# A delta-rule scan fed into a two-layer MLP on one core: the down products of the middle token groups turned round, one PSUM bank for the up products, four banks for the scan's pieces, and the last stores from two queues

## The chip, the cores and the metric

The kernel runs on one core of a Trainium2 chip. The metric is device microseconds of one execution, the median of several; lower is better. The engines are TensorE (PE in the profile; PEld is its weight load), VectorE (DVE), ScalarE (ACT), GpSimd (POOL) and SyncE (SP), which issues most of the DMAs.

## The reference

Four batches of eight heads run a delta rule over 768 steps with a state of 48x48. The outputs, 3072 tokens of 384 numbers, go through an MLP with 2048 hidden units.

```python
k_n = k / (np.linalg.norm(k, axis=-1, keepdims=True) + 1e-06)
for t in range(S):
    y[:, :, t] = einsum('bhd,bhde->bhe', q[:, :, t], state)
    v_old = einsum('bhde,bhd->bhe', state, kt)
    state = state + bt[:, :, :, None] * einsum('bhd,bhe->bhde', kt, vt - v_old)
x = y.transpose(0, 2, 1, 3).reshape(B * S, H * D)        # 3072 x 384
h = x @ w_in                                             # 384 -> 2048
g = np.where(h >= 1, h, np.where(h <= -1, 0.0, (h + 1) ** 2 / 4))
return g @ w_out                                         # 2048 -> 384
```

## The kernel before

The scan is cut into 12 chunks of 64 steps, taken in six pairs, G = 0 to 5. For each chunk there are Gram products (`gram_k`, `gram_q`), a triangular solve (16x16 blocks for the first two pairs, `solve_whole` with 30 steps of two DVE instructions, L325 and L327, for the others), merges of the solved blocks (`merge16`, `merge32`), and a chain over the state (`chain_r`, `chain_u`, `chain_y`, `chain_d`). Each of these is called a piece: a batch of some 64 small matmuls, and an eviction of their banks on ACT or DVE.

The MLP works on the 512 tokens of a pair in 16 items, one for each block `f` of 128 hidden units; pair 0 does some blocks in halves of 256 tokens and has 22. An item is:

- up: nine matmuls of 128x512 (three blocks of `x`, each as high x high, high x low and low x high parts in fp32r) into a bank `h`
- the activation, which with s = relu(0.5 - 0.5h), then relu(1 - s), then its square, then max with h gives g: three ACT instructions (L762 twice, L789) and one on DVE (L791)
- the split of g into `ghi` (ACT, L757) and `glo` (DVE, L758)
- down, two items later (`LAG = 2`): twelve matmuls of 128x384, in which the pieces of g are the weights and the block's `w_out` moves, summed over the 16 items in four banks `o0` to `o3`, one for 128 tokens.

The order on every engine is written out by hand. The loop over `items` issues the up products, then the pieces that the table `pe` holds for this half item, then the DVE and ACT work of the table `fill` (solver steps, transposes, loads), then the down products of two items ago, then the second half item's pieces ("late"). `plan(G)` fills both tables; the scan of pair G+1 runs beside the MLP of pair G, and `at(pe, G, 4.5, ...)` means the second half of item 4. An engine carries out its instructions in that order. The solver's steps for pair G+1 stand in the last items of pair G-1 and the first eight of pair G; merges and chain follow.

PSUM has eight banks: two for `h`, four for `o`, and two, called `ch`, for all pieces. When pair 0 starts and before, a ring `spare` lets the pieces use banks that the MLP doesn't need yet.

A finished pair is stored by `store`: four ACT copies and eight DMAs of 64 rows on SP. In the last pair two of the copies are on DVE, and seven of the eight DMAs are on SP, one on ACT's queue.

Of the kernel before, what the change touches and what calls it, by code (L numbers as in the profile page):

```python
# [19 lines left out]
DF = 2048  # L20
FT = DF // 128
# [3 lines left out]
PASSES = ((0, 0), (0, 1), (1, 0))  # L25
# [5 lines left out]
def delta_rule_moe(ctx: ExitStack, tc: tile.TileContext, kqa, kqb, kv, beta, w, out):  # L31
# [27 lines left out]
    ctx.enter_context(tc.manual_schedule())  # L59

    K, KE, GE, Q, KV, XB, RAW, WT = {}, {}, {}, {}, {}, {}, {}, {}
    START = [dict(name=n, bufs=b) for n, b in (("ch", 2), ("ch", 2), ("h", 2), ("h", 2), ("o2", 1), ("o3", 1), ("o0", 1), ("o1", 1))]
    spare = []

    def acc():
# [151 lines left out]
    def gram_q(g):  # L217

        x, b_ = Q[g], banks(C)
        for j in range(H):  # L220
            for e, f in quarters():
                r, o = slice(f * C, f * C + D), other(e, f) * C
                nc.tensor.matmul(b_[e][o:o + C, j], K[g][r, e * H + j, :], x[r, (1 - f, 1)[e], e * H + j, :], start=True, stop=True)  # L223

        def moved():
            for o in range(2):
                yield x[o * C:o * C + C, o, 0:H], b_[0][o * C:o * C + C], slice(o * C, o * C + C)
            yield x[:, 0, H:NU], b_[1], slice(0, P)

        def evict():  # L230
            def raw():
                for a, b, r in moved():
                    nc.scalar.copy(out=a, in_=b)

            def masks(copied=False):
                for a, b, r in moved():
                    nc.vector.tensor_tensor(out=a, in0=a if copied else b, in1=mask[r, None, :].broadcast_to([r.stop - r.start, H, C]), op=ALU.mult)  # L237
                    yield
            return (raw, masks(True)) if g < 2 else lambda: run(masks())
        return evict  # L240
# [387 lines left out]
        return slice(bs[0] * NB, bs[-1] * NB + NB)  # L628

    def up(G, f, bs):  # L630
        h = ps.tile([P, 2 * NB], F32, name="h", bufs=2)
        n = 0
        for k in range(3):
            for x, y in PASSES:
                nc.tensor.matmul(h[:, cols(bs)], WT[f][:, 0, x, k * P:(k + 1) * P], XB[G][:, y, k, cols(bs)], start=(n == 0), stop=(n == 8))  # L635
                n += 1
        return h

    def down(G, f, bs):
        ghi, glo = gs.pop((G, f, bs))  # L640
        for b in bs:
            left[G, b] -= 1
            for k in (2 * b, 2 * b + 1):
# [5 lines left out]
                for n, (x, y) in enumerate(PASSES):  # L649
                    nc.tensor.matmul(oacc[G, k], (ghi, glo)[x][:, k * P:(k + 1) * P], WT[f][:, 1, y, :],  # L650
                                     start=(new and n == 0), stop=(left[G, b] == 0 and n == 2))

    def store(G, b):
        o = sb.tile([P, 2, DM], F32, name="wx", bufs=2)
        for k in (2 * b, 2 * b + 1):
            (nc.scalar.copy, nc.vector.tensor_copy)[k % 2 if G == NS - 1 else 0](out=o[:, k % 2], in_=oacc[G, k])
            for j in range(CT):
                (nc.scalar if G == NS - 1 and k + j == TT else nc.sync).dma_start(out=out.rearrange("(b n t) m -> n b t m", b=CB, t=C)[2 * G + b, k % 2 * CT + j], in_=o[j * C:j * C + C, k % 2])
# [10 lines left out]
    def chain(G, t, a):  # L669
        for j, f, g in ((0, chain_u, a), (0.5, chain_y, a), (1.5, chain_d, a), (2.5, chain_r, a + 1), (3.5, chain_u, a + 1), (4, chain_y, a + 1), (5, chain_d, a + 1)):  # L670
            if (f, g) != (chain_d, ntot - 1):
                at(pe, G, t + j, lambda f=f, g=g: f(g))

    def plan(G):

        a, b = 2 * G + 2, 2 * G + 3
        if G == NS - 1:
            return
        va, vb = scale_v(a), scale_v(b)
        if G == 0:  # L680
# [24 lines left out]
            last = FT + HALF
        else:
            so, un = solves.pop(G)
            at(fill, G, 0.5, (va, 1))
            at(fill, G, 1, (va, 1))
            at(pe, G, 2.5, lambda: chain_r(a))  # L710
            at(pe, G, 4.5, lambda: gram_q(a))
            at(pe, G, 6, lambda: gram_q(b))
            cost, hs = 0, 0
            t, n = (-2.5, 19) if G == 1 else (-1.5, 17)
            for j in range(1, 31):
                at(fill, G, t + hs / 2, (so, 1))
                cost += j * (31 - j) + 150
                hs = int(cost / 9461 * n)
            for j, t in enumerate((7, 7.5, 8, 8)):
                at(fill, G, t, (un, 1))  # L720
            at(fill, G, 9, (vb, 1))
            at(fill, G, 9.5, (vb, 1))
            M = 8.5
            last = 16
        for j, x in ((0, (0, None)), (0.5, (1, 0)), (2.5, (None, 1))):
            at(pe, G, M + j, lambda x=x: merge32(*x))
        chain(G, M + 1.5, a)
        if G < NS - 2:
            if G:
                at(fill, G, 6.5, (load_k, a + 2))  # L730
            at(fill, G, M + 0.5, (load_k, b + 2, (nc.sync, nc.sync), True))
            at(pe, G, M + 1, lambda: gram_k(a + 2))
            at(pe, G, M + 3.5, lambda: gram_k(b + 2))
            lane_steps(G, M + 2, lanes(G + 2), 2.5, 3, 3.5, 4)
            solves[G + 1] = solve_whole(), unlanes_whole()
            at(fill, G, M + 3, (load_q, a + 2))
            at(fill, G, M + 5, (load_k, b + 2))
            at(fill, G, M + 6.5, (load_q, b + 2))
            at(fill, G, last + 0.5, (load_kv, a + 2))
            at(fill, G, last + 1.5, (load_kv, b + 2))  # L740
# [20 lines left out]
    def relu(out, in_, bias, scale):  # L761
        nc.scalar.activation(out=out, in_=in_, func=AF.Relu, bias=bias, scale=scale)  # L762

    late, last, ready = [], None, []
    for n, item in enumerate(items):
        at_, c = 2 * n, cols(item[2])
        finish(late)
        if last:
            rest(*last)
            ready.append(last[0])  # L770
        if at_ == 2 * HALF:
            spare.clear()
        h = up(*item)

        s = sb.tile([P, 2 * NB], F32, name="s", bufs=2)
        relu(s[:, c], h[:, c], mid, -0.5)
        evicts = products(*pe.pop(at_, []))
        run(wu, 3 if n == 0 else 1)
        fills(at_)
        finish(evicts)  # L780
        run(wu, 2 if n < HALF else 1)
        if len(ready) == LAG:
            x = ready.pop(0)
            down(*x)
            for b in x[2]:
                if left[x[0], b] == 0:
                    store(x[0], b)
        relu(s[:, c], s[:, c], one, -1.0)
        nc.scalar.activation(out=s[:, c], in_=s[:, c], func=AF.Square)  # L789
        late = products(*pe.pop(at_ + 1, []))  # L790
        nc.vector.tensor_tensor(out=s[:, c], in0=h[:, c], in1=s[:, c], op=ALU.max)  # L791
# [6 lines left out]
    for b in range(2):  # L798
        gs[G, FT - 1, (b,)] = gs[G, FT - 1, (0, 1)]
        down(G, FT - 1, (b,))  # L800
        store(G, b)

# [1 line left out]
def layouts(q, k, v, beta, moe_w_in, moe_w_out):  # L804
# [43 lines left out]
```

## Time and profile before

| | |
|---|---|
| time, median of 3 runs | 622.01 us (621.1 to 622.45) |
| the profiled execution's own time | 620.85 us |
| its span | 619.1 us |
| mean granted TensorE clock | 0.943 |
| PE busy | 583.6 us, 94% |
| DVE busy | 409.3 us, 66% |
| ACT busy | 393.9 us, 64% |
| time of the 16 DMA engines taken by the queue with most packets | 22.6% |

Durations that the text takes from the profile come from that one execution. A row of a timeline has the start in us from the span's start, the duration, engine, line, operation, names and shapes, and in brackets the idle time before it with what ended it. A row of groups ends with the total busy time and the mean in ns, and the idle time before. The clock is low in the first 100 us and 1.00 from about 120 us on.

### The profile page before, as it was taken

Reading aid. Unit: us, or ns where it says so; the run is one execution under the profiler, and the core shown is the slowest. Engines: PE = TensorE matmul, PEld = TensorE weight load, DVE = VectorE, ACT = ScalarE, POOL = GpSimd, SP = SyncE. Lnnn points to the kernel's source line nnn. Section 1 sums busy time; section 2 is a strip of 40 time slices with the busy share of each in tenths; the row PEclk is TensorE's granted clock in tenths of the full one; section 3 lists DMA queues with packets and bytes.
Section 4 is the critical chain, followed back from the end, with each engine's and each line's share of the span. In section 5 each row is a group of like instructions: output and inputs, shape, how many; then the busy total and the mean of one; then the engine's idle time right before and its main releaser. Section 6 shows DMA issues by size and latency. Waiting matters only on the chain.

```text
span 619.1 us, 21754 instructions
## 1 busy us (share of the span) xinstructions
PE 583.6 (94%) x9562; PEld 511.5 (83%) x9562; DVE 409.3 (66%) x848; ACT 393.9 (64%) x685; POOL 29.8 (5%) x62
## 2 busy tenths in 40 slices
PE   7977967799999999999999999999999999999996
PEld 7966956688888888888888888888888888889995
DVE  4989899972379873379973489954489945333332
ACT  3436775649667569656578646587647586666663
POOL 5110000010010000020000020000020000000000
PEclk9556697999999999999999999999999999999999
DMA  5672756200124210214210224110124000020002
GB/s 141 197 244 71 233 196 202 88 4 3 42 61 119 74 31 3 69 31 125 72 30 8 65 53 119 54 31 24 49 71 124 1 4 16 12 54 1 0 1 51
DMA packets 32831, 42.97 MB, mean 69 GB/s; under 512 B 7152, under 2 KB 27440, under 8 KB 32736
## 3 DMA queue, kind: packets, MB, share of 16 engines
q1 hardware_dynamic: 31600, 39.43, 22.6%
q10 hardware_dynamic: 880, 2.07, 1.0%
q8 instruction: 75, 1.23, 0.8%
q0 software_dynamic: 256, 0.08, 0.1%
q14 instruction: 20, 0.16, 0.1%
HBM read 34.47 MB, written 4.72 MB: 63 GB/s over the span
## 4 chain that ended last, share of the span: by engine, by line
PE 70%; ACT 11%; DVE 9%; SPq 3%; DMA 3%; issue 2%; DVEq 0%; ACTq 0%
PE o L650 27%; PE h L635 27%; PE ch L452 3%; ACT XT L406 2%; ACT GG L404 2%; PE ch L414 2%; ACT s L762 2%; PE ch L223 2%; PE ch L430 1%; ACT XT L399 1%; PE ch L496 1%; PE o L583 1%; PE ch L375 1%; ACT s L789 1%; SPq L484 1%
## 5 line engine op out<-in xcount | busy, mean ns | idle before, releaser
L635 PE MATMUL h<-xb,wt 128*128 128x512 f32 (+1 forms) x918 | 229.1, 395 | 9.1 <-DMA xb<-wt 8.1
L635 PEld LDWEIGHTS h<-xb,wt 128*128 128x128 f32 x918 | 166.8, 195 | 43.2 <-DVE xb L183 4.4
L650 PE MATMUL o<-wt,ghi 128*128 128x384 f32 x768 | 202.1, 344 | 0.1
L791 DVE TENSOR_TENSOR s<-h,s 128x512 f32<-128x512 f32 (+1 forms) x102 | 66.8, 655 | 124.3 <-ACT s L789 123.8
L650 PEld LDWEIGHTS o<-wt,ghi 128*128 128x128 f32 x768 | 137.8, 189 | 7.5 <-issue 0.5
L757 ACT CAST ghi<-s 128x512 fp32r<-128x512 f32 (+1 forms) x102 | 60.8, 597 | 110.4 <-DVE s L791 86.3
L650 PE MATMUL o<-wt,glo 128*128 128x384 f32 x384 | 130.3, 339 | 0.4 <-DVE glo L758 0.3
L762 ACT ACTIVATE s<-h,half 128x512 f32<-128x512 f32 (+1 forms) x102 | 67.5, 662 | 44.6 <-PE h L635 43.7
L758 DVE TENSOR_TENSOR glo<-s,ghi 128x512 fp32r<-128x512 f32 (+1 forms) x102 | 66.6, 653 | 34.9 <-ACT ghi L757 34.8
L650 PEld LDWEIGHTS o<-wt,glo 128*128 128x128 f32 x384 | 72.7, 189 | 1.0 <-DVE glo L758 1.0
L762 ACT ACTIVATE s<-s,one 128x512 f32<-128x512 f32 (+1 forms) x102 | 71.7, 703 | 2.4
L789 ACT ACTIVATE s<-s 128x512 f32<-128x512 f32 (+1 forms) x102 | 61.9, 607 | 3.2
L325 DVE TENSOR_TENSOR pr<-A 128x30 f32<-128x30 f32 (+14 forms) x120 | 39.3, 328 | 6.2 <-POOL A L296 4.5
L327 DVE TENSOR_TENSOR A<-A,pr 128x30 f32<-128x30 f32 (+14 forms) x120 | 39.9, 332 | 4.4
L452 PEld LDWEIGHTS ch<-Q,SU 64*64 64x64 f32 (+1 forms) x1008 | 22.1, 135 | 4.3 <-ACT ghi L757 1.5
L452 PE MATMUL ch<-Q,SU 64*64 64x64 f32 (+1 forms) x1008 | 24.3, 222 | 0.7 <-ACT SU L434 0.7
L237 DVE TENSOR_TENSOR Q<-ch,mask 64x512 f32<-64x512 f32 (+1 forms) x30 | 20.6, 688 | 0.4
L296 POOL TENSOR_SCALAR_AFFINE_SELECT A<-A 128x1024 f32<-128x1024 f32 x4 | 5.1, 1263 | 311.9 <-DMA xb<-X 258.1
L404 ACT ACTIVATE GG<-ch 32x512 f32<-32x512 f32 x22 | 13.0, 589 | 10.6 <-PE ch L392 10.3
L414 PEld LDWEIGHTS ch<-SU,K 48*64 48x64 f32 x672 | 13.2, 147 | 6.5 <-issue 4.6
L414 PE MATMUL ch<-SU,K 48*64 48x48 f32 x672 | 14.9, 232 | 3.7 <-DVE Q L237 3.7
L179 ACT ACTIVATE xb<-wt 128x768 f32<-128x768 f32 x16 | 14.5, 914 | 5.1 <-DVE wt L191 3.6
(150 smaller groups left out, 621.8 us busy)
## 6 DMA issues: line engine op xcount, KB each, us to landing
wt<-in_w_dram SPq DMA_DIRECT2D x14, 768.0 KB, 5.4
out_dram<-wx SPq DMA_DIRECT2D x47, 96.0 KB, 2.2
KV<-in_kv_dram SPq DMA_DIRECT2D x36, 96.0 KB, 2.5
KV<-in_kv_dram SPq DMA_DIRECT2D x72, 48.0 KB, 2.4
KV<-in_kv_dram SPq DMA_DIRECT2D x12, 192.0 KB, 2.7
xb<-X SPq DMA_DIRECT2D x60, 32.0 KB, 2.0
K<-in_kqb_dram SPq DMA_DIRECT2D x12, 128.0 KB, 2.7
Q<-in_kqb_dram SPq DMA_DIRECT2D x12, 128.0 KB, 2.7
```

Of the source, the lines that this page charges most:

```text
L325: nc.vector.tensor_tensor(out=pr, in0=A[:, 0:n, j:j + 1].broadcast_to([P, n, m]), in1=A[:, j:j + 1, j + 1:32].broadcast_to([P, n, m]), op= ...
L327: nc.vector.tensor_tensor(out=A[:, 0:n, j + 1:32], in0=A[:, 0:n, j + 1:32], in1=pr, op=ALU.add)
L404: nc.scalar.mul(out=GG[r:r + 32, ga, :, 0:32], in_=y1[r:r + 32], mul=-1.0)
L414: nc.tensor.matmul(b_[f][o:o + C, j], K[g][r, k, :], SU[r, (1 - f, 1)[e], k, :], start=True, stop=True)
L452: nc.tensor.matmul(yy[i][o * C:o * C + C, e, p], SF[rows, u:u + C], w_[rows, x, k, :], **how)
L635: nc.tensor.matmul(h[:, cols(bs)], WT[f][:, 0, x, k * P:(k + 1) * P], XB[G][:, y, k, cols(bs)], start=(n == 0), stop=(n == 8))
L650: nc.tensor.matmul(oacc[G, k], (ghi, glo)[x][:, k * P:(k + 1) * P], WT[f][:, 1, y, :], start=(new and n == 0), stop=(left[G, b] == 0 and n ...
L757: nc.scalar.copy(out=ghi[:, c], in_=s[:, c])
L758: nc.vector.tensor_tensor(out=glo[:, c], in0=s[:, c], in1=ghi[:, c], op=ALU.subtract)
L762: nc.scalar.activation(out=out, in_=in_, func=AF.Relu, bias=bias, scale=scale)
L789: nc.scalar.activation(out=s[:, c], in_=s[:, c], func=AF.Square)
L791: nc.vector.tensor_tensor(out=s[:, c], in0=h[:, c], in1=s[:, c], op=ALU.max)
```

## The change

It does six things.

1. In pairs 1 to 4 the down products are turned (`down_across`): the block's `w_out` is the weights, every third column of it from `k`, and the pieces of g move, so that three sums of 128 output columns x 512 tokens take nine matmuls of 512 columns. Pair 0 and pair 5 keep `down`.
2. A finished pair 1 to 4 is stored by `store_across`: six DVE transposes in blocks of 32x32 out of PSUM and sixteen DMAs on SP, with runs of 96 numbers.
3. From pair 1 on, `h` has one bank. DVE takes h out of it first, as s = max(h, -1); ACT makes q = relu(0.5 - 0.5s) and (1 - q) squared from SBUF, and DVE takes the max of s and q.
4. The banks so set free (`h1`, `o3`) join the two `ch` in a ring of four for the pieces, from item 2 of pair 1 on.
5. Five pieces a pair move to stand directly beside another: `gram_q(a)` from 4.5 to 2.5, `gram_q(b)` from 6 to 8.5, `merge32` of the second chunk, `gram_k(a + 2)` and `gram_k(b + 2)` half an item forward.
6. The last pair's stores go four to SP and four to ACT's queue (`store_last`).

```diff
-        h = ps.tile([P, 2 * NB], F32, name="h", bufs=2)
+        h = ps.tile([P, 2 * NB], F32, name="h0" if G else f"h{f % 2}")
...
+    def down_across(G, f, bs):
+        g = gs.pop((G, f, bs))
+        for b in bs:
+            left[G, b] -= 1
+        for k in range(3):
+            if f == 0:
+                oacc[G, k] = ps.tile([P, 2 * NB], F32, name=f"o{k}")
+            for n, (x, y) in enumerate(PASSES):
+                nc.tensor.matmul(oacc[G, k], WT[f][:, 1, y, k::3], g[x],
+                                 start=(f == 0 and n == 0), stop=(f == FT - 1 and n == 2))
+
+    def store_across(G):
+        o = [sb.tile([P, CT, TT, 32, 3], F32, name="wx", bufs=2) for _ in range(2)]
+        for k in range(3):
+            for x in range(2):
+                nc.vector.transpose(out=o[x][:, :, :, :, k].rearrange("p e (b h) d -> p b e h d", b=2),
+                                    in_=oacc[G, k].rearrange("p (b x n) -> p x b n", b=2, x=2)[:, x].rearrange("p b (e h d) -> p b e h d", e=CT, h=2))
+        for x in range(2):
+            for e in range(CT):
+                for i in range(4):
+                    nc.sync.dma_start(out=out.rearrange("(e n t) (i m) -> e i t n m", e=CB, t=32, i=4)[2 * x + e, i, :, 4 * G:4 * G + 4],
+                                      in_=o[x][32 * i:32 * i + 32, e].rearrange("p n d k -> p n (d k)"))
...
+    def send(G, k, j, o, q):
+        q.dma_start(out=out.rearrange("(b n t) m -> n b t m", b=CB, t=C)[2 * G + k // 2, k % 2 * CT + j], in_=o[j * C:j * C + C, k % 2])
+
+    def store_last(G):
+        o = [sb.tile([P, 2, DM], F32, name="wx", bufs=2) for _ in range(2)]
+        for k in range(TT + 1):
+            if k < TT:
+                (nc.scalar.copy, nc.vector.tensor_copy)[k % 2](out=o[k // 2][:, k % 2], in_=oacc[G, k])
+                send(G, k, 0, o[k // 2], nc.sync)
+            for x in ((0,), (), (1,), (), (2, 3))[k]:
+                send(G, x, 1, o[x // 2], nc.scalar)
...
-            at(pe, G, 4.5, lambda: gram_q(a))
-            at(pe, G, 6, lambda: gram_q(b))
+            at(pe, G, 2.5, lambda: gram_q(a))
...
+        if G:
+            at(pe, G, M, lambda: gram_q(b))
...
+        if item[:2] == (1, 2):
+            spare[:] = START[0:2] + [dict(name="h1", bufs=1), dict(name="o3", bufs=1)]
         h = up(*item)
...
+        if item[0]:
+            nc.vector.tensor_scalar(out=s, in0=h, scalar1=-1.0, scalar2=None, op0=ALU.max)
+            q = sb.tile([P, 2 * NB], F32, name="A16", bufs=1)
+            relu(q, s, mid, -0.5)
+        else:
+            relu(s[:, c], h[:, c], mid, -0.5)
...
+        if item[0]:
+            nc.scalar.activation(out=q, in_=q, func=AF.Square, bias=one, scale=-1.0)
+        else:
+            relu(s[:, c], s[:, c], one, -1.0)
+            nc.scalar.activation(out=s[:, c], in_=s[:, c], func=AF.Square)
         late = products(*pe.pop(at_ + 1, []))
-        nc.vector.tensor_tensor(out=s[:, c], in0=h[:, c], in1=s[:, c], op=ALU.max)
+        if item[0]:
+            nc.vector.tensor_tensor(out=s, in0=s, in1=q, op=ALU.max)
+        else:
+            nc.vector.tensor_tensor(out=s[:, c], in0=h[:, c], in1=s[:, c], op=ALU.max)
```

The order of the instructions at two places follows. The first is DVE, from the end of item 0 of pair 3 to item 1; `h` with a number is the up products' bank, `pr` and `A` are the solver's, `o` with a number one of pair 2's sums. Before:

```order
L758 TENSOR_TENSOR glo<-s,ghi 128x512
L258 TENSOR_TENSOR KV<-KV,N_5643 128x384
L325 TENSOR_TENSOR pr<-A 128x220
L327 TENSOR_TENSOR A<-A,pr 128x11x20
L325 TENSOR_TENSOR pr<-A 128x228
L327 TENSOR_TENSOR A<-A,pr 128x12x19
L791 TENSOR_TENSOR s<-h,s 128x512
```

And now:

```order
L794 TENSOR_TENSOR glo<-s,ghi 128x512
L815 TENSOR_SCALAR s<-h_5781 128x512
L258 TENSOR_TENSOR KV<-KV,N_5599 128x384
L325 TENSOR_TENSOR pr<-A 128x220
L327 TENSOR_TENSOR A<-A,pr 128x11x20
L325 TENSOR_TENSOR pr<-A 128x228
L327 TENSOR_TENSOR A<-A,pr 128x12x19
L668 STREAM_TRANSPOSE wx<-o_4559 128x2x2x64 x2
L668 STREAM_TRANSPOSE wx<-o_4563 128x2x2x64 x2
L668 STREAM_TRANSPOSE wx<-o_4567 128x2x2x64 x2
L843 TENSOR_TENSOR s<-s,A_5793 128x512
```

Between glo and the item's last max there is now the first max, L815, ahead of the solver's steps, and behind them the six transposes of the pair before; the last max reads SBUF alone.

The second place is ACT at `merge32` of the first and second chunk, item 9 of pair 3, now (`A` with a number is q):

```order
L798 ACTIVATE A_6284<-s,half 128x512
L399 COPY XT<-ch 32x16x32 x2
L404 ACTIVATE GG<-o_6286 32x16x32 x2
L406 COPY XT<-XT 32x16x32 x2
L214 COPY GG<-ch 128x512
L214 COPY GG<-h_6353 128x512
L837 ACTIVATE A_6284<-A_6284,one 128x512
L793 CAST ghi<-s 128x512
L798 ACTIVATE A_6432<-s,half 128x512
```

Before, these rows were:

```order
L762 ACTIVATE s<-h,half 128x512
L399 COPY XT<-ch 32x16x32 x2
L404 ACTIVATE GG<-ch 32x16x32 x2
L406 COPY XT<-XT 32x16x32 x2
L762 ACTIVATE s<-s,one 128x512
L789 ACTIVATE s<-s 128x512
L214 COPY GG<-ch 128x512 x2
L757 CAST ghi<-s 128x512
L762 ACTIVATE s<-h,half 128x512
```

The evictions of `gram_k`, L214, moved from behind the square to ahead of it, and the second relu is gone.

More of the change, by code (lines that the diff above doesn't have):

```diff
@@ L61, in delta_rule_moe @@
     K, KE, GE, Q, KV, XB, RAW, WT = {}, {}, {}, {}, {}, {}, {}, {}
-    START = [dict(name=n, bufs=b) for n, b in (("ch", 2), ("ch", 2), ("h", 2), ("h", 2), ("o2", 1), ("o3", 1), ("o0", 1), ("o1", 1))]
+    START = [dict(name=n, bufs=b) for n, b in (("ch", 2), ("ch", 2), ("h0", 1), ("h1", 1), ("o2", 1), ("o3", 1), ("o0", 1), ("o1", 1))]
     spare = []
@@ L655, in store @@
         for k in (2 * b, 2 * b + 1):
-            (nc.scalar.copy, nc.vector.tensor_copy)[k % 2 if G == NS - 1 else 0](out=o[:, k % 2], in_=oacc[G, k])
+            nc.scalar.copy(out=o[:, k % 2], in_=oacc[G, k])
             for j in range(CT):
-                (nc.scalar if G == NS - 1 and k + j == TT else nc.sync).dma_start(out=out.rearrange("(b n t) m -> n b t m", b=CB, t=C)[2 * G + b, k % 2 * CT + j], in_=o[j * C:j * C + C, k % 2])
+                send(G, k, j, o, nc.sync)
+    def send(G, k, j, o, q):
[8 more added lines that the diff above has]
+                send(G, x, 1, o[x // 2], nc.scalar)
     pe, fill = {}, {}
@@ L724, in plan @@
             last = 16
-        for j, x in ((0, (0, None)), (0.5, (1, 0)), (2.5, (None, 1))):
+        for j, x in ((0, (0, None)), (0.5, (1, 0)), (2 if G else 2.5, (None, 1))):
             at(pe, G, M + j, lambda x=x: merge32(*x))
+        if G:
+            at(pe, G, M, lambda: gram_q(b))
         chain(G, M + 1.5, a)
@@ L731, in plan @@
             at(fill, G, M + 0.5, (load_k, b + 2, (nc.sync, nc.sync), True))
-            at(pe, G, M + 1, lambda: gram_k(a + 2))
-            at(pe, G, M + 3.5, lambda: gram_k(b + 2))
+            at(pe, G, M + (0.5 if G else 1), lambda: gram_k(a + 2))
+            at(pe, G, M + (3 if G else 3.5), lambda: gram_k(b + 2))
             lane_steps(G, M + 2, lanes(G + 2), 2.5, 3, 3.5, 4)
@@ L772, in delta_rule_moe @@
             spare.clear()
+        if item[:2] == (1, 2):
+            spare[:] = START[0:2] + [dict(name="h1", bufs=1), dict(name="o3", bufs=1)]
         h = up(*item)
         s = sb.tile([P, 2 * NB], F32, name="s", bufs=2)
-        relu(s[:, c], h[:, c], mid, -0.5)
+        if item[0]:
[4 more added lines that the diff above has]
+            relu(s[:, c], h[:, c], mid, -0.5)
         evicts = products(*pe.pop(at_, []))
@@ L783, in delta_rule_moe @@
             x = ready.pop(0)
[L784 to L789, printed above, removed]
+            if 0 < x[0] < NS - 1:
+                down_across(*x)
+                if x[1] == FT - 1:
+                    store_across(x[0])
+            else:
+                down(*x)
+                for b in x[2]:
+                    if left[x[0], b] == 0:
+                        store(x[0], b)
+        if item[0]:
[3 more added lines that the diff above has]
+            nc.scalar.activation(out=s[:, c], in_=s[:, c], func=AF.Square)
         late = products(*pe.pop(at_ + 1, []))
-        nc.vector.tensor_tensor(out=s[:, c], in0=h[:, c], in1=s[:, c], op=ALU.max)
+        if item[0]:
+            nc.vector.tensor_tensor(out=s, in0=s, in1=q, op=ALU.max)
+        else:
+            nc.vector.tensor_tensor(out=s[:, c], in0=h[:, c], in1=s[:, c], op=ALU.max)
         run(wu, 2)
@@ L800, in delta_rule_moe @@
         down(G, FT - 1, (b,))
-        store(G, b)
+    store_last(G)
 def layouts(q, k, v, beta, moe_w_in, moe_w_out):
```

## The prediction

> **What bounds the kernel now.** I read the page's busy times first, then the waits of TensorE (PE) from 200 to 600 us, then a table by stretch.
>
> ```profile
> PE 583.6 (94%) x9562; PEld 511.5 (83%) x9562; DVE 409.3 (66%) x848; ACT 393.9 (64%) x685; POOL 29.8 (5%) x62
> ```
> ```profile
> PE ch L452 <- ACT SU L434: 0.7, 1, 0.7
> ```
> ```profile
> 361.19:409.40 48.21, 48.21 (x531) 42.52 (x530) 44.54 (x100) 27.91 (x45) 3.50 (x6) 1.00 0.29 77
> 409.40:450.78 41.38, 41.10 (x897) 35.08 (x896) 17.63 (x38) 31.63 (x59) 0.00 (x0) 1.00 0.12 33
> 541.00:604.00 63.00, 62.55 (x315) 56.30 (x315) 20.76 (x30) 41.20 (x65) 0.00 (x0) 1.00 0.06 14
> ```
>
> The longest wait of PE in those 400 us is 0.7 us, so PE sets the pace. The table's columns are PE, PEld, DVE, ACT, POOL, then the granted clock, which is 1.00. Its first two rows are one period of a middle pair. The reader is to see that 66% of VectorE (DVE) is an average of two halves: in the half with the solver (first row) DVE is busy 44.54 of 48.21 us, in the other 17.63 of 41.38. The timeline of DVE shows the full half closer:
>
> ```profile
> 364.51 0.19 DVE L325 TENSOR_TENSOR pr<-A 128x30 f32<-128x30 f32 x1 [1.50 <-POOL A L296]
> ...
> 373.31 0.68 DVE L791 TENSOR_TENSOR s<-h,s 128x512 f32<-128x512 f32 x1
> 373.91 0.55 DVE L258 TENSOR_TENSOR KV<-KV,N 128x384 f32<-128x384 f32 x1
> 374.38 0.37 DVE L325 TENSOR_TENSOR pr<-A 128x210 f32<-128x210 f32 x1
> 374.78 0.38 DVE L327 TENSOR_TENSOR A<-A,pr 128x210 f32<-128x210 f32 x1
> 375.08 0.68 DVE L758 TENSOR_TENSOR glo<-s,ghi 128x512 fp32r<-128x512 f32 x1
> 375.68 0.55 DVE L258 TENSOR_TENSOR KV<-KV,N 128x384 f32<-128x384 f32 x1
> ...
> 378.12 0.69 DVE L791 TENSOR_TENSOR s<-h,s 128x512 f32<-128x512 f32 x1 [0.30 <-ACT s L789]
> ...
> 398.62 2.11 DVE L237 TENSOR_TENSOR Q<-ch,mask 64x512 f32<-64x512 f32 x3
> ...
> 408.73 0.65 DVE L791 TENSOR_TENSOR s<-h,s 128x512 f32<-128x512 f32 x1
> ```
>
> One instruction starts as the last one drains: a 128x512 operation takes 0.68 us but the next starts 0.60 after it (373.31 to 373.91). From 364.51 to 409.33 (408.73 and 0.60) the only marked idle is 0.30 us. So in these 44.8 us PE and DVE are both full; DVE hides behind PE with nothing left.
>
> The second thing to read is the loop of one item where nothing else runs, in the last pair:
>
> ```profile
> 563.62 0.62 ACT L757 CAST ghi<-s 128x512 fp32r<-128x512 f32 x1 [0.81 <-DVE s L791]
> 564.88 0.69 ACT L762 ACTIVATE s<-h,half 128x512 f32<-128x512 f32 x1 [0.64 <-PE h L635]
> 565.60 0.72 ACT L762 ACTIVATE s<-s,one 128x512 f32<-128x512 f32 x1
> 566.36 0.63 ACT L789 ACTIVATE s<-s 128x512 f32<-128x512 f32 x1
> 567.80 0.62 ACT L757 CAST ghi<-s 128x512 fp32r<-128x512 f32 x1 [0.81 <-DVE s L791]
> ```
> ```profile
> 567.02 0.69 DVE L791 TENSOR_TENSOR s<-h,s 128x512 f32<-128x512 f32 x1 [2.05 <-ACT s L789]
> 568.45 0.69 DVE L758 TENSOR_TENSOR glo<-s,ghi 128x512 fp32r<-128x512 f32 x1 [0.74 <-ACT ghi L757]
> ```
> ```profile
> 562.62 2.22 PE L635 MATMUL h<-xb,wt 128*128 128x512 f32 x9
> 564.68 0.51 PE L650 MATMUL o<-wt,ghi 128*128 128x384 f32 x2
> ...
> 566.76 2.25 PE L635 MATMUL h<-xb,wt 128*128 128x512 f32 x9
> ```
>
> PE needs 2.06 us for nine matmuls of 512 columns (229 ns each) and 2.08 for twelve of 384 (173 each), 4.14 an item. ScalarE (ACT) waits 0.64 us for PE in each, so the elementwise loop has room.
>
> **The change part by part.**
>
> Down products turned: nine of 229 ns for twelve of 173, 2.06 for 2.08 us; 64 items, at most -1.3 us, and only where PE is the bound. Their weights are now read with a step of three elements. No row shows a strided weight load; I take 0 and price the other end under the rivals.
>
> The new first step on DVE, max(h, -1) out of PSUM, comes 80 times, once an item from pair 1 on. The nearest rows, and those for the transposes:
>
> ```profile
> L656 DVE COPY wx<-o 128x384 f32<-128x384 f32 x2 | 1.1, 558 | 1.5 <-PE o L650 1.5
> L181 DVE TENSOR_SCALAR xb<-xb 128x768 int32<-128x768 int32 x16 | 9.1, 566 | 0.0
> L338 DVE STREAM_TRANSPOSE GG<-XT 128x512 f32<-128x512 f32 x8 | 5.2, 689 | 0.0
> L352 DVE STREAM_TRANSPOSE XT<-A 128x512 f32<-128x512 f32 x2 | 2.0, 998 | 0.0
> ```
>
> The copy out of PSUM takes 558 ns for 384 elements, as the two-input L258 does (0.55): one element a cycle, so 0.69 us for 512, 0.60 start to start. The tensor-scalar from SBUF takes 566 for 768, twice that rate, which would make 0.43 and 0.34. I take 0.60, since the source is PSUM, and keep 0.34 as the low end; it would take 0.26 off some 43 maxes that PE waits for, and all 2.7 us of the last pair (below), 14 in all. The Trainium skill (VectorE: DVE Perf Modes, Mode 2×_2P) says that a single-source operation gets two results a cycle only out of SBUF, because PSUM has one read port; by that rule the sum keeps 0.60, with 0.34 the whole sum would be about 14 us smaller, and the copy's row agrees with the rule.
>
> ACT loses a relu (0.72) an item; the square gains a bias, which I price as the relu with one (0.72 against 0.63). ACT was not the bound, so this earns nothing by itself.
>
> But the order on DVE is now glo of item n-1, then max(h) of item n, and the single bank of h makes PE's next up products wait for that max. Behind the waiting max stand the solver's steps, which until now could run during the up products. So the whole loop is serial. In steps from start to start out of the rows above: max to ACT 0.78 (as 567.02 to 567.80), relu 0.76 (565.60 to 566.36), square 0.76, second max to ghi 0.78, ghi to glo 0.65 (567.80 to 568.45), glo to the next max 0.60: 4.33 us, against PE's 4.14. In the last pair 14 such items cost 2.7 us. With the low ends (0.34, square without extra) it is 3.97, and the cost is nothing.
>
> In the full half of pairs 2, 3 and 4, each: ten new maxes of 0.60, +6.0. Six transposes of 128x256 out of PSUM: half of 689 or 998 ns is 0.34 to 0.50; I take 0.45 start to start, +2.7 (2.0 to 3.0). They take four copies off ACT, where they cost nothing. The three masks of the later gram_q (2.11 us at 398.62, the row of L237, with the drain in it) leave the full half, -2.0. Net 6.7 us on an engine that had 0.3 free, and each item's max must come before PE's next item, so PE pays.
>
> Two places more in each of these pairs. Around the merge, ACT works without a pause:
>
> ```profile
> 412.57 1.16 ACT L399 COPY XT<-ch 32x512 f32<-32x512 f32 x2
> ...
> 417.65 1.07 ACT L214 COPY GG<-ch 128x512 f32<-128x512 f32 x2
> ```
>
> L214 now stands before the square of this item instead of behind it, 1.07 us more in the serial loop. Max (0.78) and glo (0.60) join the loop, the square grows by 0.10, and a relu (0.76) leaves it: 0.72 more. Together +1.8; at the least nothing, if PE has as much other work there. In the item in which DVE idles 1.50 us for POOL, that idle can no longer be made up by lag; PE may run ahead by one group of down products, so I take +1.0 (0 to 4). Together 6.7 + 1.8 + 1.0 = 9.5 a pair, 28.5 for three.
>
> Pair 1 has no transposes: 9 x 0.60 - 2.0 is 3.4. With 1.8 for its merge and 0.8 for places where its solver steps don't fill the gaps of the loop I take +6.0 (3.4 alone, to 9.5 as in the others).
>
> In the last pair the transposes of pair 4 stand in one item; 1.7 of the 2.7 us fit while ACT works on relu and square: +1.0.
>
> Pieces beside others: what a switch costs PE shows in the chain:
>
> ```profile
> 386.36 2.08 PE o L650 x12
> 388.44 1.09 PE ch L223 x64
> 389.53 2.26 PE h L635 x9
> 391.80 2.08 PE o L650 x12
> 393.88 2.09 PE h L635 x9
> ```
>
> The up products behind a piece take 2.26 instead of 2.09. Five pieces a pair that no longer stand alone save 0.2 each: 1.0 us a pair, 4.0 in all. Two of the five lie in the full half, where DVE now ends last, so I count three: -2.4.
>
> The queues: SP issues sixteen stores a pair instead of eight, ahead of one load of KV that is first used nine items later; nothing waits for it. The last stores:
>
> ```profile
> 612.16 4.40 SPq L658 DMA_DIRECT2D out_dram<-wx  x7
> ...
> 613.22 0.56 DVE L656 COPY wx<-o 128x384 f32<-128x384 f32 x1 [0.48 <-PE o L650]
> ...
> 613.81 0.56 ACTq L658 DMA_DIRECT2D out_dram<-wx  x1
> ```
>
> SP's seven issues take 0.63 each and the last ends at 616.56. With four on each queue, ACT's last three of 0.56 start at about 613.2 and end by 614.9: -1.7.
>
> Sum: 28.5 + 6.0 + 2.7 + 1.0 - 2.4 - 1.7 = +34.1 on the profiled 620.85 us (the span of 619.1 and 1.75 around it): 655. The -1.3 of the turned products is left out, since PE is the bound in less than half of those items. The median of the runs shown, 622.01, is 0.2% above that execution, and 0.2% is about what a measurement of this kernel can tell from no change.
>
> **The rivals.**
>
> A, faster: PE stays the bound. The max always falls into the 2.06 us of down products, the extra work of DVE is made up between items by the lag of two. Then only -1.3, -4.0 and -1.7 are left: 614. For it: DVE has 24 us free in the second half of each period. Against: instructions stand in order, and it decides where DVE's additions in the full half fit into what idles there, 0.3 us; 6.7 do not.
>
> B, slower still: the strided weight loads limit PE. The row of one now:
>
> ```profile
> L650 PEld LDWEIGHTS o<-wt,ghi 128*128 128x128 f32 x768 | 137.8, 189 | 7.5 <-issue 0.5
> ```
>
> Strided transposes cost 998 for 689, a factor of 1.45. So would 189 become 274 against a spacing of 229: 45 ns x 576 is 26 us where PE is the bound all along, and about 14 on top of my sum, since half of it hides while DVE is late: 668. The low end is 0, if the 189 ns are mostly latency. The Trainium skill (SBUF — State Buffer, Door 1: The DMA port swizzle, its note on cachelines) has lines of 16 bytes, of which at least two accesses should hit each; a step of 12 bytes gives one and a third, so by that rule the load slows. No run here shows it yet.
>
> C, the milder case: the max runs at 0.34: 34.1 less 14 is 20, 641; if PE's lead also swallows the 1.0 beside POOL and pair 1's gaps, 3.8 in all, 637.
>
> D: gains and losses cancel within 0.2%.
>
> **How the numbers follow.** Forecast 0.60 (645 to 667: transposes from 2.0 to 3.0, POOL's idle from 0 to 4, pair 1 from 3.4 to 9.5), B 0.17, C 0.12, A 0.08, D 0.03. All but A and D are slower: 0.89; faster 0.08, same 0.03. The range from 630 to 673 leaves out A, D, and the far parts of B and C, about 2 in 10.
>
> **What would show it.** In the full half the first max's row reads 0.69 us and DVE has no idle, while PE waits for DVE at the up products, some 6 to 9 us a pair. In the last pair items come every 4.33 us. The up products after the former lone pieces shrink by 0.2. Weight loads of the turned products stay near 189 ns. I am wrong if PE shows no waits for the first max, if DVE's new row reads 0.43, or if down products space wider than 229 ns with DVE idle.

## The result, and the profile after

The changed kernel takes 665.58 us (median of four runs, 662.77 to 667.22) against 621.91 for the kernel before (621.10 to 622.45): a ratio of 1.0689, 95% interval 1.0653 to 1.0726. It is slower by about 43 us; the forecast was 655, with a range of 630 to 673. The profiled execution took 664.24 us, its span is 662.5.

Busy times and the head of the chain that ended last, from the page of after:

```profile
PE 597.2 (90%) x9370; PEld 515.6 (78%) x9370; DVE 468.5 (71%) x952; ACT 342.7 (52%) x589; POOL 30.0 (5%) x62
PE 35%; DVE 34%; ACT 15%; issue 6%; DMA 4%; SPq 3%; POOL 1%; DVEq 0%; ACTq 0%; POOLq 0%
```

DVE has 59 us more work than before and ACT 51 us less, and a third of the chain runs through DVE. No engine is near 100% in the mean, and none has to be: the waits say who stands still for whom. A row has the us in total, how many times, and the longest; the first three are from PE's list, the others from the list of all engines.

```profile
PE h L635 <- DVE s L815: 15.3, 14, 2.6
PE h L635 <- issue: 5.1, 2, 2.6
PE o L661 <- DVE wx L668: 1.6, 3, 0.5
...
ACT A L798 <- DVE s L815: 151.5, 77, 4.8
DVE s L843 <- ACT A L837: 93.2, 58, 6.2
```

PE now waits at the up products for the first max, L815, as forecast. The two waits of 2.6 us put down to "issue" are of the same kind: the one at 388.82 ends 0.1 us after the end of a max that ran from 388.04 for 0.68. In each of pairs 2 to 4 these waits come to 5.0 to 5.3 us.

The full half on DVE, at the turn from item 0 to item 1 of pair 3 (timeline of DVE):

```profile
397.99 0.68 DVE L794 TENSOR_TENSOR glo<-s,ghi 128x512 fp32r<-128x512 f32 x1
398.59 0.68 DVE L815 TENSOR_SCALAR s<-h 128x512 f32<-128x512 f32 x1
399.19 0.55 DVE L258 TENSOR_TENSOR KV<-KV,N 128x384 f32<-128x384 f32 x1
399.66 0.38 DVE L325 TENSOR_TENSOR pr<-A 128x220 f32<-128x220 f32 x1
400.07 0.39 DVE L327 TENSOR_TENSOR A<-A,pr 128x220 f32<-128x220 f32 x1
400.50 0.40 DVE L325 TENSOR_TENSOR pr<-A 128x228 f32<-128x228 f32 x1
400.93 0.40 DVE L327 TENSOR_TENSOR A<-A,pr 128x228 f32<-128x228 f32 x1
401.24 2.26 DVE L668 STREAM_TRANSPOSE wx<-o 128x256 f32<-128x256 f32 x6
403.39 0.64 DVE L843 TENSOR_TENSOR s<-s,A 128x512 f32<-128x512 f32 x1
403.95 0.38 DVE L325 TENSOR_TENSOR pr<-A 128x234 f32<-128x234 f32 x1
404.37 0.40 DVE L327 TENSOR_TENSOR A<-A,pr 128x234 f32<-128x234 f32 x1
404.77 0.69 DVE L794 TENSOR_TENSOR glo<-s,ghi 128x512 fp32r<-128x512 f32 x1
```

No row has an idle time in brackets. An item takes 6.78 us here, from glo to glo.

Where the 43 us arise can be read from the same instruction in both kernels. The glo of items 13 of pair 2, 2 and 8 of pair 3, and 13 of pair 3, before (L758) and after (L794):

```profile
356.46 0.65 DVE L758 TENSOR_TENSOR glo<-s,ghi 128x512 fp32r<-128x512 f32 x1
384.03 0.69 DVE L758 TENSOR_TENSOR glo<-s,ghi 128x512 fp32r<-128x512 f32 x1
412.00 0.69 DVE L758 TENSOR_TENSOR glo<-s,ghi 128x512 fp32r<-128x512 f32 x1 [2.62 <-ACT ghi L757]
446.05 0.65 DVE L758 TENSOR_TENSOR glo<-s,ghi 128x512 fp32r<-128x512 f32 x1
```
```profile
376.72 0.67 DVE L794 TENSOR_TENSOR glo<-s,ghi 128x512 fp32r<-128x512 f32 x1
412.00 0.68 DVE L794 TENSOR_TENSOR glo<-s,ghi 128x512 fp32r<-128x512 f32 x1
441.41 0.69 DVE L794 TENSOR_TENSOR glo<-s,ghi 128x512 fp32r<-128x512 f32 x1 [0.29 <-ACT ghi L793]
477.31 0.66 DVE L794 TENSOR_TENSOR glo<-s,ghi 128x512 fp32r<-128x512 f32 x1
```

The full half (items 14, 15 and 0 to 8) takes 64.69 us instead of 55.54, +9.15; of that +7.71 falls in its first five items. The merge (items 9 to 13) takes 35.90 instead of 34.05, +1.85. The table gives the same differences for the other pairs; the steps add up to the span's +43.4.

| Stretch | after minus before, us |
|---|---|
| up to the last glo of pair 0 | -0.05 |
| pair 1: items 0 to 8, merge | 6.6, 3.7 |
| turn into pair 2 to its item 8, merge | 9.2, 0.8 |
| pair 3, the same | 9.15, 1.85 |
| pair 4, the same | 9.4, 1.2 |
| from there to the last glo | 2.8 |
| from the last glo to the end | -1.2 |

The busy times of the full half say the same (columns PE, PEld, DVE, ACT, POOL; before in two stretches, then after):

```profile
356.46:384.03 27.57, 27.57 (x335) 24.54 (x330) 24.14 (x65) 16.28 (x31) 3.50 (x6) 1.00 0.34 86
384.03:412.00 27.97, 27.97 (x426) 24.45 (x425) 24.42 (x52) 17.16 (x28) 0.00 (x0) 1.00 0.19 55
```
```profile
376.72:412.00 35.28, 31.03 (x375) 26.07 (x369) 31.37 (x80) 11.44 (x20) 3.50 (x6) 0.95 0.25 62
412.00:441.41 29.41, 27.56 (x355) 23.50 (x355) 26.59 (x54) 14.72 (x22) 0.00 (x0) 1.00 0.22 60
```

DVE is busy 57.96 us instead of 48.56, +9.4, and the half grew by 9.15. PE, full before, now idles 6.1 us of it.

### The profile page after: what moved, and what is told of

The parts are those of the page before. It is cut to its first block, busy times and chain, and to the rows that moved or that the text cites. A ratio compares the mean times of both kernels' runs of the same rounds, so it can differ in the third digit from the quotient of the medians.

```text
span 662.5 us, 21526 instructions
## 1 busy us (share of the span) xinstructions
PE 597.2 (90%) x9370; PEld 515.6 (78%) x9370; DVE 468.5 (71%) x952; ACT 342.7 (52%) x589; POOL 30.0 (5%) x62
## 4 chain that ended last, share of the span: by engine, by line
PE 35%; DVE 34%; ACT 15%; issue 6%; DMA 4%; SPq 3%; POOL 1%; DVEq 0%; ACTq 0%; POOLq 0%
PE h L635 13%; PE o L661 6%; PE o L650 5%; DVE glo L794 5%; DVE s L815 5%; ACT A L798 4%; ACT A L837 4%; DVE s L843 3%; DVE pr L325 3%; DVE A L327 3%; DVE Q L237 2%; ACT ghi L793 2%; DVE SU L511 1%; DVE XT L335 1%; DMA xb<-X 1%
## 5 line engine op out<-in xcount | busy, mean ns | idle before, releaser
L635 PE MATMUL h<-xb,wt 128*128 128x512 f32 (+1 forms) x918 | 236.1, 403 | 29.6 <-DVE s L815 15.3
L798 ACT ACTIVATE A<-s,half 128x512 f32<-128x512 f32 x80 | 57.9, 724 | 157.7 <-DVE s L815 151.5
L661 PE MATMUL o<-ghi,wt 128*128 128x512 f32 x384 | 126.1, 410 | 1.6 <-DVE wx L668 1.6
L843 DVE TENSOR_TENSOR s<-s,A 128x512 f32<-128x512 f32 x80 | 55.1, 689 | 93.5 <-ACT A L837 93.2
L661 PEld LDWEIGHTS o<-ghi,wt 128*128 128x128 f32 x384 | 92.8, 254 | 7.0 <-issue 2.9
L794 DVE TENSOR_TENSOR glo<-s,ghi 128x512 fp32r<-128x512 f32 (+1 forms) x102 | 66.6, 653 | 25.2 <-ACT ghi L793 25.0
L661 PE MATMUL o<-glo,wt 128*128 128x512 f32 x192 | 77.0, 401 | 0.0
L650 PE MATMUL o<-wt,ghi 128*128 128x384 f32 x256 | 68.1, 347 | 0.9 <-ACT ghi L793 0.8
L837 ACT ACTIVATE A<-A,one 128x512 f32<-128x512 f32 x80 | 58.0, 725 | 2.3
L815 DVE TENSOR_SCALAR s<-h 128x512 f32<-128x512 f32 x80 | 54.8, 686 | 3.9 <-PE h L635 3.8
L650 PEld LDWEIGHTS o<-wt,ghi 128*128 128x128 f32 x256 | 45.9, 190 | 3.9 <-ACT ghi L793 1.1
L650 PE MATMUL o<-wt,glo 128*128 128x384 f32 x128 | 43.7, 342 | 0.4 <-DVE glo L794 0.3
```

The lines of the kernel that those rows point to most:

```text
L661: nc.tensor.matmul(oacc[G, k], WT[f][:, 1, y, k::3], g[x], start=(f == 0 and n == 0), stop=(f == FT - 1 and n == 2))
L794: nc.vector.tensor_tensor(out=glo[:, c], in0=s[:, c], in1=ghi[:, c], op=ALU.subtract)
L815: nc.vector.tensor_scalar(out=s, in0=h, scalar1=-1.0, scalar2=None, op0=ALU.max)
L837: nc.scalar.activation(out=q, in_=q, func=AF.Square, bias=one, scale=-1.0)
L843: nc.vector.tensor_tensor(out=s, in0=s, in1=q, op=ALU.max)
```

## The experiments

Three theories stood at the start. **Q**: what costs is the first max in DVE's row in the full half, and the serial loop behind it. **W**: the stepped weight loads limit PE. **B**: one bank for the up products as such makes PE wait, whoever frees it. A ratio is always against runs of the kernel before in the same series, whose medians lay between 621.1 and 622.2 us.

**ACT frees the bank.** Everything else of the change stays.

```diff
-            nc.vector.tensor_scalar(out=s, in0=h, scalar1=-1.0, scalar2=None, op0=ALU.max)
+            relu(s, h, one, 1.0)
...
-            relu(q, s, mid, -0.5)
+            relu(q, s, one, -0.5)
...
-            nc.vector.tensor_tensor(out=s, in0=s, in1=q, op=ALU.max)
+            nc.vector.scalar_tensor_tensor(out=s, in0=s, scalar=-1.0, in1=q, op0=ALU.add, op1=ALU.max)
```

> The changed kernel, but the single bank of h is freed by ScalarE, as u = relu(h + 1), then q = relu(1 - u/2), (1 - q) squared, and VectorE only takes max(u - 1, that). VectorE has one instruction of 0.69 us less an item, the loop leaves VectorE's glo out: 0.72 + 0.76 + 0.76 + 0.78 + 0.65 = 3.67 us, under PE's 4.14. Theory Q: PE is the bound again, 620.85 - 4.0 (fewer switches) - 1.7 (last stores) + up to 2, so 614 to 622. Theory W: nothing of PE's cost changes, 650 or more. Theory B (one bank for h as such stalls PE, whoever empties it): 645 or more.

Measured: 630.38 us, ratio 1.0129 (1.0109 to 1.0149). One instruction moved from DVE to ACT takes back 35 us of the 43. Of PE's list of waits, the row that takes the place of the 15.3 us:

```profile
PE h L635 <- ACT s L798: 4.3, 7, 1.6
```

B is refuted as the main cause, since the bank is as single as before. But some 8 us are left, more than Q had allowed (622 at most).

**The max on DVE alone.** The kernel before with the new activation from pair 1 on; two banks, old products, old places.

```diff
-        relu(s[:, c], h[:, c], mid, -0.5)
+        if item[0]:
+            nc.vector.tensor_scalar(out=s, in0=h, scalar1=-1.0, scalar2=None, op0=ALU.max)
+            q = sb.tile([P, 2 * NB], F32, name="A16", bufs=1)
+            relu(q, s, mid, -0.5)
...
```

> The kernel before with the new activation alone (VectorE takes max(h, -1) first), two banks for h, old down products, old places of the pieces, old stores. Theory Q: 6.0 us more in each of three full halves, about 4 in pair 1, 0.72 at each merge and 2.7 in the last pair: about +28, 645 to 655. Theory B and theory W: no more than a few us, 620 to 627.

Measured: 670.73 us, ratio 1.0767 (1.0739 to 1.0795). The new activation by itself costs as much as the whole change, and with two banks. Q was right in direction and 16 us too low in size. So the single bank is not needed for the cost. With two banks PE's list names no wait for the first max; its long waits stand elsewhere, and the kernel before has neither of these rows:

```profile
PE ch L392 <- DVE XT L335: 11.7, 4, 3.1
PE o L650 <- ACT wx L656: 7.5, 4, 2.3
```

What the two kernels have in common is DVE's row: item 15 of pair 2 and items 0, 3 and 5 of pair 3, in which DVE has the same instructions in both, take 5.89, 4.67, 4.33 and 4.74 us from glo to glo in both. That the part costs 5 us more than the whole was not expected either. In the profiled runs the difference is 10.3 us: 2.2 lie ahead of pair 1, where the two kernels do the same, and 7.1 in the merges of pairs 2 to 4, which cost 2.9, 2.9 and 5.2 us here. Why they do is open.

**The max on DVE only where DVE has room.** In the changed kernel ACT frees the bank in items 0 to 8, 14 and 15 of pairs 1 to 4, as in the first experiment, and DVE in the others.

```diff
+            acts = item[0] < NS - 1 and (item[1] < 9 or item[1] > 13)
+            if acts:
+                relu(s, h, one, 1.0)
+            else:
                 nc.vector.tensor_scalar(out=s, in0=h, scalar1=-1.0, scalar2=None, op0=ALU.max)
...
```

> The changed kernel, in which ScalarE frees the bank in items 0 to 8, 14 and 15 of pairs 1 to 4 (beside the solver, where DVE is full), and DVE still frees it in items 9 to 13 and in the whole last pair (36 of 80 items). Theory Q (the first max costs where DVE's row is full): of the 35 us between DVE-first and ScalarE-first everywhere only the last pair's 2.6 and up to 4 in the merges come back: 633 to 637 us. Theory L (the longer loop through DVE costs in every item alike): 36/80 of 35 us come back: 646.

Measured: 635.07 us, ratio 1.0208 (1.0170 to 1.0246). This is the run that places the cost: with DVE still first in 36 of 80 items only about 5 of the 35 us come back. Q holds, and L, a cost in every item alike, is refuted.

**Weights without a step.** The turned products read `WT[f][:, 1, y, k * P:(k + 1) * P]`, so the output's columns come in another order.

> The changed kernel, but the turned down products read 128 neighbouring columns of the weights instead of every third one (so the output's columns are in another order). Theory Q (VectorE's queue: the first max stands in a serial loop and adds to a full queue): PE is not the bound, the spacing of 233 ns falls to about 229 and at most 2 to 4 us go: 661 to 666 us. Theory W (strided weight loads limit PE, 254 ns instead of 190): some 26 us go, about 640.

Measured: 664.75 us, ratio 1.0668 (1.0634 to 1.0701), not to be told from the changed kernel's 1.0689. The groups of weight loads: first three of after (turned products in two rows, straight ones in the last), then one of this experiment.

```profile
L661 PEld LDWEIGHTS o<-ghi,wt 128*128 128x128 f32 x384 | 92.8, 254 | 7.0 <-issue 2.9
L661 PEld LDWEIGHTS o<-glo,wt 128*128 128x128 f32 x192 | 48.7, 254 | 0.6
L650 PEld LDWEIGHTS o<-wt,ghi 128*128 128x128 f32 x256 | 45.9, 190 | 3.9 <-ACT ghi L793 1.1
```
```profile
L661 PEld LDWEIGHTS o<-ghi,wt 128*128 128x128 f32 x384 | 71.6, 191 | 20.4 <-issue 3.8
```

The step does slow a load, from 190 to 254 ns. The turned products, in groups of three, start every 0.70 us in after (396.87, 397.57, 398.27 in pair 3), which is 233 ns each, for the 229 of the up products before the change. Without the step they start every 0.70 us as well (387.80, 388.50, 389.20 in this run), so the slower load does not reach them. W is refuted as a cause. The same edit on the kernel in which ACT frees the bank, where PE is busy for 54.9 of the 57.0 us of pair 3's full half again:

> ScalarE frees the bank, new places, and the turned products read their weights without a step (output columns in another order). With PE the bound again, a stepped load could now show: the turned matmuls were spaced 233.5 ns instead of 229, 4.5 ns x 576 = 2.6 us, so 627 to 628. If all of it hides still: 630 to 631.

Measured: 628.98 us, ratio 1.0121 (1.0099 to 1.0144) for 1.0129. The intervals overlap almost wholly; the 2.6 us that I had worked out from the spacing are not seen. They could not be: the spacing is 233 ns without the step too. A smaller gain can't be told from none.

**Six copies on ACT for the six transposes on DVE.** The output isn't put in order.

```diff
-                nc.vector.transpose(out=o[x][:, :, :, :, k].rearrange("p e (b h) d -> p b e h d", b=2),
-                                    in_=oacc[G, k].rearrange("p (b x n) -> p x b n", b=2, x=2)[:, x].rearrange("p b (e h d) -> p b e h d", e=CT, h=2))
+                nc.scalar.copy(out=o[x].rearrange("p e t n d -> p (e t n d)")[:, k * 256:k * 256 + 256], in_=oacc[G, k][:, x * 256:x * 256 + 256])
```

> The changed kernel, with the six DVE transposes of a pair's sums replaced by six ScalarE copies of the same size (the output is not put in order). Theory Q1 (every instruction added to DVE's row in its full half is paid by PE, the transposes with it): 3 pairs x 6 x 0.38 to 0.45 us = 7 to 8, and 1 for the last pair: 656 to 658 us. Theory Q2 (the first max that PE waits for is what costs, and the transposes fall where DVE would have waited for ScalarE anyway): 663 us or more.

Measured: 660.67 us, ratio 1.0641 (1.0595 to 1.0688), about 3 us less than the changed kernel by the ratios, with intervals that overlap. Neither theory's number came out. The full half of pair 3 in this run:

```profile
373.18:407.77 34.59, 29.37 (x375) 25.15 (x369) 29.26 (x73) 12.97 (x26) 3.50 (x6) 1.00 0.27 65
407.77:437.13 29.36, 27.57 (x355) 23.55 (x355) 26.54 (x55) 14.71 (x22) 0.00 (x0) 1.00 0.22 57
```

DVE has 2.16 us less work than in after, the half is 0.74 shorter (63.95 for 64.69). So of the 2.3 us of transposes a third is paid here. In pairs 2 and 4, where the half is 1.0 and 1.3 us shorter, about a half is. The item behind them in pair 3 (400.55 to 407.77, glo to glo) keeps the 7.22 us that it has in after.

**Work for PE in its waits.** Ahead of the up products of items 0 and 4 of pairs 2 to 4, eight matmuls whose result nobody uses.

```diff
+        if 2 <= item[0] <= 4 and item[1] in (0, 4):
+            idle = ps.tile([P, 2 * NB], F32, **spare[0])
+            for _ in range(8):
+                nc.tensor.matmul(idle, WT[0][:, 0, 0, 0:P], XB[item[0] - (item[1] == 0)][:, 0, 0, :], start=True, stop=True)
         h = up(*item)
```

The reason was this: in after, nine up products behind a wait of over 2 us often took 3.05 to 3.88 us instead of 2.25 to 2.37; three of the six places:

```profile
388.82 3.69 PE L635 MATMUL h<-xb,wt 128*128 128x512 f32 x9 [2.56 <-issue]
...
413.33 2.35 PE L635 MATMUL h<-xb,wt 128*128 128x512 f32 x9 [2.24 <-DVE s L815]
...
513.91 3.63 PE L635 MATMUL h<-xb,wt 128*128 128x512 f32 x9 [2.23 <-DVE s L815]
```

> The changed kernel, with eight matmuls of 512 columns (1.9 us in all, their result is not used) ahead of the up products of items 0 and 4 of pairs 2 to 4, where PE waits 2.2 to 2.6 us for the first max. They keep PE at work in the wait. Theory K (the slower clock after such a wait, 3.05 to 3.88 us for nine products instead of 2.35 in four of these places, is paid by the whole loop): 4.3 us less in all, 661 us, and no row of nine up products above 2.5 us after these waits. Theory D (DVE's row alone sets the pace, and PE's slow products are made up): 664 to 667 with the clock at 1.00 all the same.

Measured: 664.59 us, ratio 1.0714 (1.0672 to 1.0757). The same places in pair 4:

```profile
494.79 2.34 PE L635 MATMUL h<-xb,wt 128*128 128x512 f32 x9 [0.71 <-issue]
...
519.29 2.35 PE L635 MATMUL h<-xb,wt 128*128 128x512 f32 x9 [0.36 <-DVE s L819]
```

The slow products are gone at all six places (2.34 to 2.35 us), and nothing is won: by the glo rows the first five items of the full half cost +7.7 us in each of the three pairs, to the tenth as in after. Theory D holds at these places. The clock also fell in the merges of this run (0.76 to 0.90 of full between 340 and 360 and between 440 and 460), so its total loss was not removed. What a slower clock costs there can be read from the merges of all profiled runs that have the changed kernel's merge (after, the run without a step, the one with copies, and this one). Over the kernel before, nine merges with a mean clock of 1.00 cost 0.55 to 1.23 us, three at 0.95 cost 1.85 to 2.65, and four at 0.91 cost 3.5 to 3.7. So a slow clock that DVE hides in the full half is paid in the merge, with some 2.5 us where it fell furthest.

**The places of the pieces.** Two kernels in which ACT frees the bank: in the first only `gram_k` and the last merge piece go back to their former places,

```diff
-        for j, x in ((0, (0, None)), (0.5, (1, 0)), (2 if G else 2.5, (None, 1))):
+        for j, x in ((0, (0, None)), (0.5, (1, 0)), (2.5, (None, 1))):
...
-            at(pe, G, M + (0.5 if G else 1), lambda: gram_k(a + 2))
+            at(pe, G, M + 1, lambda: gram_k(a + 2))
-            at(pe, G, M + (3 if G else 3.5), lambda: gram_k(b + 2))
+            at(pe, G, M + 3.5, lambda: gram_k(b + 2))
```

> The same, but only the two gram_k and the last merge piece are back at their former places; both gram_q stay beside other pieces. Theory P: 624 to 627 us, if gram_k's eviction ahead of the square is the part that costs. If gram_q(b) in the merge costs as well, less is gained: 627 to 630. Theory T: 630 to 632.

and in the second both `gram_q` as well (4.5 and 6).

> ScalarE frees the bank as in the experiment before, and all pieces of pairs 1 to 4 are back at their former places. What is left over the kernel before (630.4 against 621.9) is to be told apart. Theory P (the new places stretch the merge, where ScalarE's evictions now stand ahead of the square): 621 to 625 us. Theory T (the transposes on DVE and the stepped weights are what is left, and lone pieces cost PE 0.2 each again): 631 to 635.

Measured: 626.57 us, ratio 1.0081 (1.0062 to 1.0101), and 628.40, ratio 1.0107 (1.0084 to 1.0130). So the new places in the merge cost 3 to 4 us (1.0129 to 1.0081), and `gram_q` beside other pieces seems to save 1.6, which would be eight pieces of 0.2 us, though these two intervals overlap. The first run came out where P put it; the second lies between the two theories, so the places are a part of what is left and not all of it.

P's number came out, but the rows do not bear out its mechanism. By the glo rows of the profiled runs the merges of pairs 1 to 4 cost 1.9, 4.4, -0.2 and 0.3 us over the kernel before with the new places, and 0.6, 0.6, 0.6 and 1.1 with the former. The gain lies in pairs 1 and 2 alone. There, at the new place, PE has a gap of 1.8 to 2.0 us in the middle of `gram_k`, for which the profile names no releaser, and in pair 2 the merge's mean clock is 0.96; with the former place there is no such gap. In pair 3, which has the same order on ACT and no gap, the new place is the shorter one. What ends the gap is open. The one in pair 2:

```profile
330.36 0.27 PE L210 MATMUL h<-K 48*64 48x64 f32 x1 [1.95 <-issue]
```

The first of these edits on the changed kernel itself:

> The changed kernel, with both gram_k and the last merge piece at their former places. With ScalarE freeing the bank this gave 3.9 us. Theory P (ScalarE's eviction ahead of the square lengthens the serial loop in the merge, about 1 us a pair): 661 to 663. Theory N (with DVE freeing the bank, DVE's row sets the pace there too and the places don't matter): 665 to 667.

Measured: 667.45 us, ratio 1.0744 (1.0713 to 1.0774). Nothing is won here; N holds, though the time is 0.45 us above its range. Its profiled run is 3.3 us longer than that of after, and 2.5 of these lie ahead of pair 1, where the two programs are alike.

**Straight products.** ACT frees the bank, merge places as before, and `down` with its four ACT copies in every pair; the ring has three banks and `gram_q(a)` is alone again.

> ScalarE frees the single bank, merge pieces at their former places, and the down products of all pairs as before the change (twelve of 384 columns, four ScalarE copies, no transposes), so the ring has three banks; of the pieces beside others only gram_q(b) stays, gram_q(a) is alone again. 626.6 with turned products. Theory T (what is left over the kernel before is the turned products: transposes ahead of the first max, products 4.5 ns apart more): 620 to 623. Theory S (it is the single bank, which makes PE wait for ScalarE's first step): 626 to 629.

Measured: 623.51 us (six runs), ratio 1.0039 (1.0018 to 1.0059). The turned products with their transposes cost some 2 to 3 us of what was left, close to what T says (620 to 623). What remains is 2.4 us over the kernel before, although the new last stores are in this kernel too; which part of the change that is, no run tells.

**The last stores alone**, in the kernel before.

> The kernel before with the new last stores alone (four DMAs on each of two queues). From the page: the last issue moves from 616.6 to 614.9, so 1.7 us less, 620.0 to 620.5. If the landing time is what counts and the queues interfere: no change.

Measured: 620.50 us (twelve runs), ratio 0.9977 (0.9965 to 0.9988). It is the one part of the change that is shown to pay by itself, and the fastest version that was run.

## Why the prediction was right, and where it was off

The mechanism was right in its main step, and the runs show it: DVE's row was full beside the solver, the first max had to go through it, and PE waited. One step of it was not needed: the single bank does make PE wait for the max in the changed kernel, but the new activation costs no less with two banks. The sum came out 9 us short of the span's difference (34.1 for 43.4). The largest misses are the full half of pairs 2 to 4, pair 1 and the switches. Term by term:

- **The first max.** Forecast 0.69 us out of PSUM, measured 686 ns. Rival C falls. The Trainium skill (VectorE: DVE Perf Modes, Mode 2×_2P) has two results a cycle only for sources in SBUF; the row of 686 ns agrees.

```profile
L815 DVE TENSOR_SCALAR s<-h 128x512 f32<-128x512 f32 x80 | 54.8, 686 | 3.9 <-PE h L635 3.8
L668 DVE STREAM_TRANSPOSE wx<-o 128x256 f32<-128x256 f32 x24 | 9.1, 474 | 0.0
```

- **The full half of pairs 2 to 4**: 7.7 forecast (6.7 and 1.0 for POOL), 9.2 measured, three times over, +4.5. By the glo rows of pair 3, 0.6 of the 1.5 us is an eleventh item, where I had counted ten. The seven items with neither transposes nor moved masks cost 6.0 us over the kernel before, for 5.2 (0.60 each, and POOL's 1.0). The other four came out as forecast, 3.2 for 3.1, but by luck. The transposes cost less than their 2.7: six run from 401.24 to 403.39, 0.36 from start to start for my 0.45, and taking them out gave 0.74 to 1.3 a pair. The credit of 2.0 for the masks of `gram_q(b)` was smaller too: item 6, which they left, takes 4.38 us for 5.14, when one more max and 2.0 less would have made 3.74; 4.38 is close to the 4.33 of the last pair's loop, which may be what holds it; no run shows that.
- **The merge**: 1.8 forecast, 0.8, 1.85 and 1.2 in pairs 2 to 4. In pair 1 it cost 3.7. There PE has a gap of 2.11 us in the middle of `gram_k`, for which the profile names no releaser, and behind it the clock is at 0.66 for ten us. The run without a step has the same gap in pair 1, a clock of 1.00 behind it, and a merge that costs 0.9; so the 2.8 us between them go with the clock. First after, then, in the last fence, that run:

```profile
242.30 0.26 PE L210 MATMUL ch<-K 48*64 48x64 f32 x1 [2.11 <-issue]
```
```profile
240.00:245.00 5.00, 2.89 (x50) 2.36 (x42) 1.13 (x3) 3.84 (x7) 0.00 (x0) 0.66 0.02 5
245.00:250.00 5.00, 5.00 (x16) 3.81 (x14) 1.85 (x3) 2.85 (x5) 0.00 (x0) 0.66 0.00 0
```
```profile
241.59 0.21 PE L210 MATMUL ch<-K 48*64 48x64 f32 x1 [2.11 <-issue]
239.00:244.00 5.00, 2.89 (x71) 2.42 (x66) 1.42 (x3) 3.56 (x6) 0.00 (x0) 1.00 0.02 5
```

- **Pair 1**: 6.0 forecast, 10.3 measured: 6.6 for 4.2 in its full half, and this merge.
- **Fewer switches**: -2.4 forecast, and not to be found. The 0.2 us a piece fits where ACT frees the bank (1.6 us for eight `gram_q`, with intervals that overlap), but in the changed kernel DVE sets the pace in the full half, and putting the merge's pieces back wins nothing there (667.45 us).
- **The last pair**: 4.33 us an item forecast; measured, from max to max, 4.33:

```profile
629.67 0.68 DVE L815 TENSOR_SCALAR s<-h 128x512 f32<-128x512 f32 x1
634.00 0.68 DVE L815 TENSOR_SCALAR s<-h 128x512 f32<-128x512 f32 x1
```

  With the transposes of pair 4 it cost 2.8 for the 3.7 forecast. The last stores gave -1.2 in the profile and -1.7 between the medians of the two kernels, for -1.7.

Rival A falls with the waits, rival B with the run without a step. B's price for a load was not far off (254 ns for 274), but it does not reach the matmuls. The Trainium skill (SBUF — State Buffer, Door 1: The DMA port swizzle, its note on cachelines) asks for two accesses to each 16-byte line; a step of 12 bytes has fewer, and the load's row agrees in direction, with no price in time. One of the signs that I had named failed with it: that these loads stay near 189 ns. The turned products do space wider than 229 ns, which I had named, with DVE idle, as a sign of being wrong, but by 4 ns and without the step too. PE's waits for the max were 5.0 to 5.3 us a pair for 6 to 9, and DVE, which I had without idle time, idles 4.4 us of the full half of pair 3, 1.8 of them in waits for the square.

## What to carry to other kernels

Look at the busy share by stretch before work is moved to an engine with room in the mean: DVE had a third of its time free, but none of it beside the solver, and there one short instruction an item, at the head of a serial loop, cost some 30 us. With two buffers the cost was no smaller, since the engine's row was the limit and not the buffer. An instruction that every item needs belongs on an engine with room in that stretch, and which engine that is may change from one stretch to the next. A slow stretch of the engine that waits, such as PE's lower clock after a wait, cost nothing where another engine set the pace, and went with up to 2.8 us a merge where it did not.

## What was not expected of the hardware

- A weight load of 128x128 whose columns lie three elements apart takes 254 ns for 190, and yet products of 512 columns with such weights go on every 233 ns, as they do without the step.
- After waits of 2.2 to 2.6 us PE's next nine products took 3.05 to 3.88 us in four of six such places and 2.35 in two. With eight matmuls put into the wait all six took 2.34 to 2.35. Without them the slow ones were three of six in the run without a step and one of six in the run with copies, so six places are few to judge by.
- Up to the last glo of pair 0, where all these kernels do the same, the profiled runs differ by -0.8 to +2.4 us from before.
- Transposes of 128x256 out of PSUM follow each other every 0.36 us on DVE, although one reads 474 ns.
